# An FFT-mixing and channel-mix kernel on one Trainium2 core: mu's rows reordered behind the first sines, turn's rows on ScalarE, the feature sine first, the first half of the features ahead in two K pieces

## The chip, the cores and the metric

The kernel runs on one core of one Trainium2 chip. Its time is the device time of one execution in microseconds (us). The kernel before took a median of 431.68 us over three runs (431.59 to 433.62). A profile is one execution taken by the hardware profiler; its times count from the span's start. PE is TensorE (PEld its weight loads), DVE is VectorE, ACT is ScalarE, POOL is GpSimd, SP is SyncE, and "L757" is line 757 of the kernel.

## The reference

The input x has 8 batches of 3072 rows with 256 features. The first part is the real part of a two-dimensional Fourier transform, over the rows and over the features. The second part mixes each row of that result with the row before it, by two vectors mu_k and mu_r, and applies a gated two-layer block:

```python
X = np.fft.fft(x, axis=1)
X = np.fft.fft(X, axis=2)
x = X.real
...
xk = mu_k * x + (1.0 - mu_k) * x_prev
xr = mu_r * x + (1.0 - mu_r) * x_prev
k = np.maximum(xk @ w_k, 0.0)
v = k * k @ w_v
r = 1.0 / (1.0 + np.exp(-(xr @ w_r)))
return (r * v).astype(np.float32)
```

w_k is 256 x 1024, w_v is 1024 x 256 and w_r is 256 x 256. The result has x's shape, in float32.

## The kernel before, in words

**Transform.** The row transform is factored: x is loaded in strips and its mirrored strips are gathered by index (`load_p`, `load_m`; GpSimd issues nearly all of these transfers), both are added on VectorE (`fold`, lines 171 and 173), and TensorE multiplies the sums by a table of sines and cosines, `w_pm` (`a_sum`, line 582). `a_evac` copies the products out of PSUM as the tile `a`. Then comes the feature transform with the table `w_eo` (`d_units`, line 604; evicted as `g_all`), then the last factor of the row transform with the table `m_cs` (`c_sums`, line 646; evicted as `y`). A small permutation matrix, `turn`, mirrors one column of features (`turned`, line 627).

**Tables.** The tables are made on the chip in the first microseconds. Rows of small whole numbers are built on VectorE from an index ramp and multiplied out on TensorE as outer products (lines 334). VectorE turns the products into angles and wraps them (`ts`, line 265, used everywhere for tensor_scalar), and ScalarE takes the sine: lines 386 and 388 for `w_pm`, line 440 (`m_sine`) for `m_cs` in two parts, line 486 (`eo_sine`) for `w_eo`. The angles of the second part of `m_cs` are made on ScalarE (`m_angles_2`, line 396) and wrapped on VectorE. Line 839 then makes ScalarE load the function table with Sigmoid, which all later work uses. Two rows, TO and SG, stand in the tile `rw_turn` and become columns from which `turn` is made.

**mu.** The vectors mu_k and mu_r come by two small transfers into `mu_row`. The features sit on the partitions in the order even, odd, and mirrored for the second half, so mu is put in that order by copies on ScalarE (`mu_rows`, line 226) into `mu_p`, and TensorE turns the rows into columns (line 843).

**Mixing and the block.** `diff` subtracts neighbouring rows; `mix_part` adds mu times the difference to y. It does so either in one scalar_tensor_tensor for each half a of the features (line 738), or in two steps, `scaled` (line 711) and `mixed` (line 722). The feature contraction of w_k is in two pieces of 128, a = 0 and a = 1 (the K pieces). `k_products` (line 757) multiplies x by w_k, `k_piece` evicts with a Relu (line 767), `square` squares it on VectorE (line 777), `v_part` and `v_tile` multiply by w_v (lines 810 and 798), `r_item` makes the gate (lines 784 and 789), and `v_out` multiplies both and stores (line 820).

**Order.** Each engine's order is the program's order, pinned by `pin_order`. PSUM tiles come from two rings, three large ones (`ps_w`) and two small ones (`ps_v`); a tile can be written again when its last reader is done. The first chunk is special: its first 256 columns of `k_products` come ahead of the main loop, and of these the first four rows are mixed directly out of PSUM (lines 887 and 892). `keep_busy` (line 206) issues matmuls on zeros to fill pauses of TensorE. After the prologue, a loop of steps runs a planned list of work items.

Of the kernel before, what the change touches and what calls it, by code (L numbers as in the profile page):

```python
# [9 lines left out]
FP32 = mybir.dt.float32  # L10
# [3 lines left out]
AF = mybir.ActivationFunctionType  # L14
# [6 lines left out]
def _v(ap, extra_offset, free_dims):  # L21
    new_ap = [list(ap.ap[0])] + [[s, c] for (s, c) in free_dims]
    return dataclasses.replace(ap, offset=ap.offset + extra_offset, ap=new_ap)
# [16 lines left out]
def kernel(  # L40
# [10 lines left out]
    nc = tc.nc  # L51
# [3 lines left out]
    P = 128  # L55
# [3 lines left out]
    NJ, NJ1 = 14, 6  # L59

    const = ctx.enter_context(tc.tile_pool(name="const", bufs=1))
# [16 lines left out]
    def ps_w():  # L78
        return ps_slot("W", 3, 1024)

    def ps_v():
        return ps_slot("V", 2, 512)
# [23 lines left out]
    V = nc.vector  # L106
# [96 lines left out]
    def keep_busy(n, ps, cols=512):  # L203

        for _ in range(n):
            nc.tensor.matmul(out=ps[:, 0:cols], lhsT=zeros,
                             rhs=_v(zeros, 0, [(0, cols // P), (1, P)]), start=True, stop=True)
# [6 lines left out]

    nc.sync.dma_start(out=xp_32, in_=dataclasses.replace(x[0, 0:1, :],
                                                         ap=[[32 * D, 96], [D, 5], [1, D]]))
    mu_row = const.tile([2, 256], FP32)
    mu_p = const.tile([2, 2, P], FP32)
    unit = const.tile([2, 2], FP32)
    for i, mu in enumerate((moe_mu_k, moe_mu_r)):  # L220
        nc.scalar.dma_start(out=mu_row[i:i + 1], in_=mu.rearrange("(a b) -> a b", a=1))

    def mu_rows(a):
        for p0, f0, step, n in (((0, 0, 1, 1), (1, 2, 2, 63), (64, 1, 2, 64)),
                                ((0, 128, 1, 1), (1, 254, -2, 63), (64, 255, -2, 64)))[a]:
            nc.scalar.activation(out=mu_p[:, a, p0:p0 + n], in_=_v(mu_row, f0, [(step, n)]),
                                 func=AF.Copy)

    for h in range(2):
# [33 lines left out]
    def ts(out, in0, s1, op0, s2=None, op1=None):  # L263
        kw = {} if op1 is None else {"op1": op1}
        V.tensor_scalar(out=out, in0=in0, scalar1=s1, scalar2=s2, op0=op0, **kw)

    MUL, ADD = ALU.mult, ALU.add
# [9 lines left out]
    TO, SG = range(2)  # L277
# [5 lines left out]
    def rv(n, o, *dims, k=1):  # L283
        return _v(rw_0[0:k], P * n + o, list(dims)) if n < 6 else _v(rw_1, P * (n - 6) + o, list(dims))

    def tv(n, o, *dims):
        return _v(rw_turn, P * n + o, list(dims))

    one = ramp[0:1]
    C_0, C_1 = [(64, 2), (1, 32)], [(64, 2), (1, 32)]  # L290
# [7 lines left out]
    V.memset(rv(PH0, 64 + 47, (1, 1)), -S / 4)  # L298
    V.memset(rv(PHS0, 64 + 15, (1, 1)), S / 4)
    V.memset(rv(ONE, 0, (1, 1)), 1.0)  # L300

# [8 lines left out]
    for i in range(2):  # L312
        nc.scalar.activation(out=unit[:, i:i + 1], in_=g_i[0:2], func=AF.Copy, bias=1.0 - i,
                             scale=2.0 * i - 1.0)
    mu_rows(0)
    mu_rows(1)

    ts(rv(JR, 0, (1, P)), one, 0.0, ADD)
    ts(rv(PN, 0, (2, 64), (1, 2)), _v(one, 0, [(2, 64), (0, 2)]), 0.0, ADD)
# [49 lines left out]
    ts(ph_c, prep[:, P_C:P_C + 4], float(TURN) / S, MUL)  # L369


    V.memset(tv(SG, 0, (1, P)), 1.0)
    V.memset(tv(SG, 32, *C_1), -1.0)
    V.memset(tv(SG, 47, (64, 2)), 1.0)
    for c in range(2):
        ts(tv(TO, 32 * c, (64, 2), (1, 32)), _v(one, 32 * c, [(64, 2), (1, 32)]),
           32.0 - 64.0 * c, ADD)
    ts(tv(TO, 15, (32, 4)), _v(one, 15, [(32, 4)]), 0.0, ADD)

    ang_ps = [ps_v(), ps_v()]  # L380
    m_outer(ang_ps[0], 0, NJ1)
# [2 lines left out]
    for g in range(2):  # L384
        kw = dict(func=AF.Sin, bias=sc[:, 2 + g:3 + g], scale=sc[:, g:g + 1])
        nc.scalar.activation(out=_v(w_pm, g, [(WA + WB, 2), (2, 2), (4, NU)]),
                             in_=_v(u_w, 0, [(0, 2), (NU, 2), (1, NU)]), **kw)
        nc.scalar.activation(out=_v(w_pm, WA + g, [(WA + WB, 2), (2, NU)]),
                             in_=_v(u_w, 2 * NU, [(0, 2), (1, NU)]), **kw)

    def wrap_angles(j0, j1):
        ts(ang[:, :, j0:j1], ang[:, :, j0:j1], TURN - 1, ALU.bitwise_and)

    def m_angles_2(ps, j0, j1):
        for c in range(2):
            nc.scalar.activation(out=ang[:, c, j0:j1], in_=ps[:, 0:64 * (j1 - j0)],  # L396
                                 func=AF.Identity, bias=ph_c[:, 2 * c:2 * c + 1],
                                 scale=float(TURN) / S)

    def m_angles(ps, j0, j1, z=0):  # L400
        for c in range(2):
            for k0, k1, n in ((j0, j0 + z, 2 * c + 1), (j0 + z, j1, 2 * c))[1 - z:]:
                ts(ang[:, c, k0:k1], ps[:, 64 * (k0 - j0):64 * (k1 - j0)], float(TURN) / S, MUL,
                   ph_c[:, n:n + 1], ADD)
        if j0 == 0:
            wrap_angles(j0, j1)

    m_angles(ang_ps[0], 0, NJ1, 1)
    for c in range(2):
        ts(ueo[:, :, c], _v(prep, P_E, [(64, 2), (1, 64)]), TURN / 256.0, MUL,  # L410
           0.75 * (1 - c) * TURN, ADD)
    ts(ueo, ueo, TURN - 1, ALU.bitwise_and)
    keep_busy(NF[0], fill)

    turn = const.tile([P, P], FP16)
# [69 lines left out]
    def eo_sine():  # L485
        nc.scalar.activation(out=w_eo.rearrange("p a b -> p (a b)"),
                             in_=ueo.rearrange("p a c b -> p (a c b)"), func=AF.Sin,
                             bias=m_pi, scale=TWO_PI / TURN)
# [108 lines left out]
    def d_units(b, ps, u0, n, bank):  # L597

        for i in range(n):
            for e in range(2):
                o = bank * e + 128 * i
                nc.tensor.matmul(out=ps[:, o:o + 128],  # L604
                                 lhsT=a_t[b][:, e, 2 * (u0 + i):2 * (u0 + i) + 2, :],
                                 rhs=w_eo[:, e], start=True, stop=True)

    def d_evac(ps, u0, n, bank, eng):
        evac(_v(g_all, 256 * u0, [(64, 2), (128, 2 * n), (1, 64)]),
             _v(ps, 0, [(bank, 2), (64, 2 * n), (1, 64)]), eng)  # L610
# [8 lines left out]
    def d_small(b, u, n, eng="A"):  # L619
        ps = ps_v()  # L620
        d_units(b, ps, u, n, 256)
        d_evac(ps, u, n, 256, eng)
# [35 lines left out]
    def y_evac(b, s0, n, ps):  # L658
        o = s0 % 2
        evac(y_t[b][:, s0:s0 + n].rearrange("p s a t -> p (s a t)"),  # L660
             _v(ps, 512 * o, [(128, n // 2), (512 - 1024 * o, 2), (1, 128)]), "A")
# [62 lines left out]
                        op=ALU.subtract if m else ALU.add)  # L724

    def mix_part(b, j, lo, hi):
        if j or lo > 4:
            for a in range(2):
                scaled(b, j, 0, a, lo, hi)
            for a in range(2):  # L730
                mixed(b, j, 0, a, lo, hi)
            return


        if lo == 0:
            x_t[b, j, 0] = mix_pool.tile([P, 2, 1536], FP16, name=f"x{j}0")
        for a in range(2):
            V.scalar_tensor_tensor(out=_v(x_t[b, j, 0], 1536 * a + 64 * lo,
                                          [(64, hi - lo), (1, 64)]),
                                   in0=x_t[b][:, lo:hi, a], scalar=mu_f[:, a, j:j + 1],  # L740
                                   in1=y_t[b][:, lo:hi, a], op0=ALU.mult, op1=ALU.add)
# [4 lines left out]

    k2_t, st = {}, {}

    def k_products(c, ds, lo=0, hi=512):
        b, m, i = c  # L750
        xk = x_t[b, 0, m]
        if lo == 0:
            st["k", ds] = ps_w()
        for hs in range(2):
            fc = 2 * ds + hs
            for a in range(2):
                nc.tensor.matmul(out=st["k", ds][:, 512 * hs + lo:512 * hs + hi],  # L757
                                 lhsT=wk_sb[m][a][:, 128 * fc:128 * fc + 128],
                                 rhs=xk[:, a, 512 * i + lo:512 * i + hi],
                                 start=(a == 0), stop=(a == 1))  # L760

    def k_piece(c, ds):
        if ds == 0:
            k2_t[c] = k2_pool.tile([P, 8, 512], FP16, name="k2", tag="k2")
            st["rl"] = k2_pool.tile([P, 8, 512], FP16, name="rl", tag="rl")
        k_products(c, ds, 256 if c == chunks[0] and ds < 2 else 0)
        nc.scalar.activation(out=st["rl"][:, 2 * ds:2 * ds + 2],  # L767
                             in_=st["k", ds].rearrange("p (f t) -> p f t", f=2),
                             func=AF.Relu, bias=0.0, scale=0.25)
# [59 lines left out]

    m_angles_2(ang_ps[1], NJ1, NJ)
    ts(w_pm[:, 0:2, WA:WA + WB], w_pm[:, 0:2, WA:WA + WB], math.sqrt(0.5), MUL)
    ts(w_pm[:, 2], w_pm[:, 0], -1.0, MUL)
    wrap_angles(NJ1, NJ)
    m_sine(0, NJ1)
    eo_sine()
    m_sine(NJ1, NJ)
    nc.scalar.activation(out=warm, in_=zeros[:, 0:1], func=AF.Sigmoid)  # L839
    fold(0, 0, 1, 4)  # L840
# [30 lines left out]
    w, first = ps_w(), ps_w()  # L871
# [13 lines left out]
    for a in range(2):  # L885
        t = x_t["t", a] = mix_pool.tile([P, 24, 64], FP16, name=f"t{a}")
        nc.scalar.activation(out=t[:, 0:4],
                             in_=_v(first, 64 * a, [(128, 2), (512, 2), (1, 64)]), func=AF.Copy,
# [39 lines left out]
    chunks = [(b, m, i) for b in range(B) for m in range(2) for i in range(3)]  # L928
# [16 lines left out]
    for n, c in enumerate(chunks[:EARLY]):  # L945
        o_steps[4 * n + SHORT + 3] = [(c, 1, 2), (c, 3, 2)]
    o_steps[4 * EARLY + SHORT + 3] = [(chunks[EARLY], 1, 2)]
    k_products(chunks[0], 0, 0, 256)
    k_products(chunks[0], 1, 0, 256)
    diff(0, 4, 8)  # L950
    mix_part(0, 0, 4, 8)
    d_small(0, 8, 2)
    d_small(0, 10, 2)
    y_evac(0, 0, 4, first)
    diff(0, 8, 16)
    at(0, mix_part, 0, 0, 8, 16)
    at(0, diff, 0, 0, 4)
# [71 lines left out]
    for b in range(B):  # L1029
# [9 lines left out]
        if t < B:  # L1039
# [6 lines left out]
            c = [(c_pairs, t, 8 * n, (8, 8, 8, 4)[n], EV[n]) for n in range(4)]  # L1046
# [75 lines left out]
```

## Time and profile before

| what | value |
| --- | --- |
| median of three runs | 431.68 us (431.59 to 433.62) |
| profiled execution, its own time | 431.61 us |
| its span | 429.8 us |
| busy share of the span | PE 98%, DVE 84%, ACT 74%, POOL 15% |
| granted TensorE clock | 1.000 |
| moved by DMA | 42.06 MB, mean 98 GB/s |

The span runs from the first to the last instruction; 1.8 us of the profiled execution's time lie around it. In the views that follow, a row of a timeline begins with its start and its length in us, then engine, line, operation, the tiles written and read, shapes and count; consecutive equal instructions are merged into one row, and the bracket at the end says how long the engine was idle before and what ended that. A row of the chain of waits begins with start and length of a link. A row of waits reads: who waited, for whom, us in total, times, longest. A row of DMA issues ends with the time from issue to landing. A row of groups reads: count, busy us in all, mean ns of one, idle before.

### The profile page before, as it was taken

To read this page: it belongs to the slowest core of one execution; us is meant where nothing else is said; L and a number is where in the kernel's file an instruction comes from. 1 tells how busy PE (TensorE), PEld (TensorE's weight loads), DVE (VectorE), ACT (ScalarE), POOL (GpSimd) and SP (SyncE) were. 2 spreads that over 40 slices of the span, in tenths; PEclk is the share of its full clock that TensorE was granted. 3 is DMA by queue.
4 is the path that set the end of the run, shared out by engine and by line. 5 is a ranking of instruction groups with operands and counts; after the bars stand their busy time and mean duration, and the time that the engine had idled before them with its cause. 6 is when DMAs were issued, how large, how long until landed. Compare 5 with 4: busy or idle time off the path is not lost.

```text
span 429.8 us, 9301 instructions
## 1 busy us (share of the span) xinstructions
PE 422.9 (98%) x3858; PEld 298.0 (69%) x3858; DVE 360.9 (84%) x547; ACT 320.2 (74%) x373; POOL 63.4 (15%) x96
## 2 busy tenths in 40 slices
PE   8999999999999999999999999999999999999996
PEld 3667776777777776776677777777767767766765
DVE  8899989997998889988898988989799847997453
ACT  7889897877878678776777777777786767666661
POOL 7686302000050002300041000500000000000000
PEclk9999999999999999999999999999999999999999
DMA  8999917322286233933269223763232322223233
GB/s 169 134 152 207 231 48 129 76 56 68 71 147 150 51 76 63 191 93 72 58 115 188 57 55 72 135 157 75 53 72 50 76 64 61 70 64 72 67 74 98
DMA packets 35103, 42.06 MB, mean 98 GB/s; under 512 B 4115, under 2 KB 31093, under 8 KB 35061
## 3 DMA queue, kind: packets, MB, share of 16 engines
q1 hardware_dynamic: 27488, 25.41, 23.7%
q0 software_dynamic: 7264, 15.80, 22.5%
q8 instruction: 30, 0.49, 0.5%
q10 hardware_dynamic: 308, 0.26, 0.2%
q14 instruction: 13, 0.10, 0.1%
HBM read 32.08 MB, written 25.17 MB: 133 GB/s over the span
## 4 chain that ended last, share of the span: by engine, by line
PE 94%; ACT 3%; DVE 1%; DMA 1%; issue 0%; ACTq 0%
PE psW L757 39%; PE psV L798 36%; PE psW L784 10%; PE psV L810 3%; PE psW L604 2%; PE psW L678 1%; PE psW L564 1%; DMA mu_row<-in_moe_mu_r_dram 1%; PE psW L646 1%; ACT a L521 1%; ACT m_cs L440 0%; PE psW L582 0%; ACT L839 0%; DVE x L892 0%; ACT rl L396 0%; ACT rl L767 0%
## 5 line engine op out<-in xcount | busy, mean ns | idle before, releaser
L767 ACT ACTIVATE rl<-psW 128x1024 f16<-128x1024 f32 x192 | 195.2, 1025 | 92.5 <-PE psW L757 89.0
L757 PE MATMUL psW<-x,wk 128*128 128x512 f16 (+1 forms) x776 | 195.7, 377 | 0.5
L798 PE MATMUL psV<-wv_sb,k 128*128 128x256 f16 x1424 | 184.1, 273 | 0.0
L798 PEld LDWEIGHTS <-k 128*128 128x128 f16 x1424 | 136.8, 98 | 35.9
L777 DVE TENSOR_TENSOR k<-rl 128x2048 f16<-128x2048 f16 (+1 forms) x101 | 116.3, 1152 | 33.4 <-ACT rl L767 33.0
L757 PEld LDWEIGHTS <-wk 128*128 128x128 f16 x776 | 74.8, 98 | 53.5 <-issue 1.3
L820 DVE SCALAR_TENSOR_TENSOR o<-psV,r 128x512 f32<-128x512 f32 (+1 forms) x97 | 65.8, 681 | 15.1 <-PE psV L798 13.5
L722 DVE TENSOR_TENSOR x<-y,t 128x1536 f16<-128x1536 f16 (+2 forms) x72 | 61.6, 860 | 2.1
L784 PE MATMUL psW<-wr,x 128*128 128x256 f16 x384 | 49.8, 273 | 0.0
L789 ACT ACTIVATE r<-psW 128x1024 f16<-128x1024 f32 x48 | 48.9, 1019 | 0.8 <-PE psW L784 0.8
L784 PEld LDWEIGHTS <-x 128*128 128x128 f16 x384 | 37.4, 98 | 14.4 <-issue 0.2
L463 POOL IOTA gate<- 1x1 int32 x6 | 2.1, 356 | 199.4 <-DVE gate L462 199.4
L521 ACT ACTIVATE a<-psW 128x832 f16<-128x832 f32 x31 | 25.9, 862 | 1.4 <-PE psW L564 1.4
L521 ACT ACTIVATE g_all<-psW 128x1024 f16<-128x1024 f32 (+5 forms) x37 | 25.6, 695 | 0.4 <-PE psW L627 0.2
L140 POOL DMA_INDIRECT xm<-in_x_dram,idx_g x18 | 24.2, 1344 | 5.5 <-issue 5.5
L171 DVE TENSOR_TENSOR p<-xp,xm 112x2304 f16<-112x2304 f16 (+6 forms) x19 | 21.6, 1139 | 0.0
L711 DVE TENSOR_SCALAR t<-d,muf_t 128x1536 f16<-128x1536 f16 (+2 forms) x40 | 20.8, 529 | 0.0
L711 DVE TENSOR_SCALAR t<-d,mu_m 128x1536 f16<-128x1536 f16 x32 | 19.6, 614 | 0.0
L604 PEld LDWEIGHTS <-a 128*128 128x128 f16 x208 | 14.0, 98 | 6.6 <-ACT a L521 0.6
L182 DVE TENSOR_TENSOR eo<-p 112x1152 f16<-112x1152 f16 (+3 forms) x28 | 17.9, 679 | 0.0
L521 ACT ACTIVATE pq<-psW 128x1024 f16<-128x1024 f32 (+1 forms) x18 | 15.2, 879 | 2.3 <-PE psW L678 2.3
L699 DVE TENSOR_TENSOR d<-y 128x1664 f16<-128x1664 f16 (+5 forms) x19 | 16.7, 880 | 0.0
(137 smaller groups left out, 217.7 us busy)
## 6 DMA issues: line engine op xcount, KB each, us to landing
out_dram<-o SPq DMA_DIRECT2D x189, 128.0 KB, 2.4
xp<-in_x_dram POOLq DMA_DIRECT2D x12, 216.0 KB, 4.5
xp<-in_x_dram POOLq DMA_DIRECT2D x13, 192.0 KB, 7.4
xp<-in_x_dram POOLq DMA_DIRECT2D x2, 384.0 KB, 6.9
wv_sb<-in_moe_w_v_dram POOLq DMA_DIRECT2D x1, 512.0 KB, 8.2
xp<-in_x_dram SPq DMA_DIRECT2D x1, 480.0 KB, 4.7
xp<-in_x_dram POOLq DMA_DIRECT2D x1, 432.0 KB, 6.4
xm<-in_x_dram,idx_g POOLq DMA_INDIRECT x18, 7.9
```

The source lines that it names most:

```text
L140: nc.gpsimd.indirect_dma_start(dst, None, src, bass.IndirectOffsetOnAxis(ap=idx, axis=0))
L521: nc.scalar.activation(out=out_ap, in_=in_ap, func=AF.Copy)
L604: nc.tensor.matmul(out=ps[:, o:o + 128], lhsT=a_t[b][:, e, 2 * (u0 + i):2 * (u0 + i) + 2, :], rhs=w_eo[:, e], start=True, stop=True)
L711: V.tensor_scalar(out=dst, in0=src, scalar1=mu, scalar2=None, op0=ALU.mult)
L722: V.tensor_tensor(out=_v(x_t[b, j, m], o, [(64 * step, hi - lo), (step, 64)]), in0=y_t[b][:, lo + 3 * m:hi + 3 * m, a], in1=x_t["t", a][:, ...
L757: nc.tensor.matmul(out=st["k", ds][:, 512 * hs + lo:512 * hs + hi], lhsT=wk_sb[m][a][:, 128 * fc:128 * fc + 128], rhs=xk[:, a, 512 * i + l ...
L767: nc.scalar.activation(out=st["rl"][:, 2 * ds:2 * ds + 2], in_=st["k", ds].rearrange("p (f t) -> p f t", f=2), func=AF.Relu, bias=0.0, sca ...
L777: V.tensor_tensor(out=k2_t[c][:, lo:hi], in0=r, in1=r, op=ALU.mult)
L784: nc.tensor.matmul(out=ps[:, 256 * tb:256 * tb + 256], lhsT=x_t[b, 1, m][:, a, 512 * i + 128 * tb: 512 * i + 128 * tb + 128], rhs=wr_sb[m] ...
L789: nc.scalar.activation(out=st["r", c], in_=ps, func=AF.Sigmoid)
L798: nc.tensor.matmul(out=st["v", tb - h][:, 256 * h:256 * h + 256], lhsT=k2_t[c][:, fc, 128 * tb:128 * tb + 128], rhs=wv_sb[:, fc], start=(f ...
L820: V.scalar_tensor_tensor(out=o.rearrange("p a b -> p (a b)")[:, 0:256 * n], in0=st["v", t0][:, 0:256 * n], scalar=16.0, in1=st["r", c][:, ...
```

## The change

Six edits, all ahead of or at the very beginning of the main loop:

- `mu_row` is one column wider. `mu_rows` is three copies instead of six: one copies mu's element 128 behind the row's end, then one strided copy for each half writes all 128 values. It is called behind the sines of `w_pm`, ahead of `m_angles_2`, where it stood ahead of them.
- SG's three memsets on VectorE stand earlier, with the other rows; TO's three rows are made on ScalarE instead of VectorE.
- VectorE makes the feature angles `ueo` ahead of `m_angles`, and wraps the second part's angles ahead of the scaling of `w_pm`; ScalarE takes the feature sine ahead of `m_cs`.
- `mix_part` for rows 4 to 8 of the first chunk uses two scalings and two additions instead of two scalar_tensor_tensor.
- The first 256 and the second 256 columns of the first two `k_products` of the first chunk are issued by K piece: a = 0 for both PSUM tiles, then a = 1. In the second 256 columns the last piece of the second tile stands behind the first tile's Relu in the program.
- `y_evac(0, 0, 4, first)` is issued ahead of two `d_small` instead of behind them.

```diff
-    mu_row = const.tile([2, 256], FP32)
+    mu_row = const.tile([2, 257], FP32)
...
-        nc.scalar.dma_start(out=mu_row[i:i + 1], in_=mu.rearrange("(a b) -> a b", a=1))
-
-    def mu_rows(a):
-        for p0, f0, step, n in (((0, 0, 1, 1), (1, 2, 2, 63), (64, 1, 2, 64)),
-                                ((0, 128, 1, 1), (1, 254, -2, 63), (64, 255, -2, 64)))[a]:
-            nc.scalar.activation(out=mu_p[:, a, p0:p0 + n], in_=_v(mu_row, f0, [(step, n)]),
+        nc.scalar.dma_start(out=mu_row[i:i + 1, 0:256], in_=mu.rearrange("(a b) -> a b", a=1))
+    def mu_rows():
+        nc.scalar.activation(out=mu_row[:, 256:257], in_=mu_row[:, 128:129], func=AF.Copy)
+        for a in range(2):
+            nc.scalar.activation(out=mu_p[:, a], in_=_v(mu_row, 256 * a, [(1 - 2 * a, 2),
+                                                                         (2 - 4 * a, 64)]),
                                  func=AF.Copy)
...
+    V.memset(tv(SG, 0, (1, P)), 1.0)
+    V.memset(tv(SG, 32, *C_1), -1.0)
+    V.memset(tv(SG, 47, (64, 2)), 1.0)
...
-    mu_rows(0)
-    mu_rows(1)
...
-    V.memset(tv(SG, 0, (1, P)), 1.0)
-    V.memset(tv(SG, 32, *C_1), -1.0)
-    V.memset(tv(SG, 47, (64, 2)), 1.0)
     for c in range(2):
-        ts(tv(TO, 32 * c, (64, 2), (1, 32)), _v(one, 32 * c, [(64, 2), (1, 32)]),
-           32.0 - 64.0 * c, ADD)
-    ts(tv(TO, 15, (32, 4)), _v(one, 15, [(32, 4)]), 0.0, ADD)
+        nc.scalar.activation(out=tv(TO, 32 * c, (64, 2), (1, 32)),
+                             in_=_v(one, 32 * c, [(64, 2), (1, 32)]), func=AF.Copy,
+                             bias=32.0 - 64.0 * c)
+    nc.scalar.activation(out=tv(TO, 15, (32, 4)), in_=_v(one, 15, [(32, 4)]), func=AF.Copy)
...
-    m_angles(ang_ps[0], 0, NJ1, 1)
     for c in range(2):
         ts(ueo[:, :, c], _v(prep, P_E, [(64, 2), (1, 64)]), TURN / 256.0, MUL,
            0.75 * (1 - c) * TURN, ADD)
     ts(ueo, ueo, TURN - 1, ALU.bitwise_and)
+    m_angles(ang_ps[0], 0, NJ1, 1)
...
-        if j or lo > 4:
+        if j or lo:
...
-    def k_products(c, ds, lo=0, hi=512):
+    def k_products(c, ds, lo=0, hi=512, halves=(0, 1)):
...
-        if lo == 0:
+        if lo == 0 and halves[0] == 0:
...
-            for a in range(2):
+            for a in halves:
...
+    def k_early(lo, hi, which):
+        for a, ds in which:
+            k_products(chunks[0], ds, lo, hi, (a,))
...
-        k_products(c, ds, 256 if c == chunks[0] and ds < 2 else 0)
+        if c == chunks[0] and ds < 2:
+            if ds == 0:
+                k_early(256, 512, ((0, 0), (0, 1), (1, 0)))
+            else:
+                k_early(256, 512, ((1, 1),))
+        else:
+            k_products(c, ds)
...
+    mu_rows()
     m_angles_2(ang_ps[1], NJ1, NJ)
+    wrap_angles(NJ1, NJ)
     ts(w_pm[:, 0:2, WA:WA + WB], w_pm[:, 0:2, WA:WA + WB], math.sqrt(0.5), MUL)
     ts(w_pm[:, 2], w_pm[:, 0], -1.0, MUL)
-    wrap_angles(NJ1, NJ)
+    eo_sine()
     m_sine(0, NJ1)
-    eo_sine()
     m_sine(NJ1, NJ)
...
-    k_products(chunks[0], 0, 0, 256)
-    k_products(chunks[0], 1, 0, 256)
+    k_early(0, 256, ((0, 0), (0, 1), (1, 0), (1, 1)))
     diff(0, 4, 8)
     mix_part(0, 0, 4, 8)
+    y_evac(0, 0, 4, first)
     d_small(0, 8, 2)
     d_small(0, 10, 2)
-    y_evac(0, 0, 4, first)
```

## The prediction

> **What bounds the kernel now.** I read the page first, then the chain of waits over the first 50 us, then the waits, and last each engine's order of time and the DMA landings.
>
> ```profile
> span 429.8 us, 9301 instructions
> PE 94%; ACT 3%; DVE 1%; DMA 1%; issue 0%; ACTq 0%
> ...
> PEld L810 <- DVE k L777: 0.5, 1, 0.5
> ```
>
> The chain that ends last runs on TensorE for 94% of the span. The whole edit lies ahead of that stretch, so it is worth only what it moves the moment at which TensorE stops waiting. The chain of waits says where that is (start, length, what):
>
> ```profile
> 7.00 1.12 ACT rl L396 x2
> ...
> 10.40 1.28 ACT L839
> ...
> 17.38 1.13 DVE x L892 x4
> ...
> 20.41 0.93 PE psW L757 x7
> ...
> 23.32 1.05 PE psV L810 x8
> ```
>
> Read naively, ScalarE carries the first part, and everything taken off it is gain. The wait row above warns against that for the end of the stretch: the last thing that TensorE waits for in the prologue is the square on VectorE in front of the matmuls of line 810 at 23.32.
>
> **The sines move forward.** ScalarE sat still for 1.10 us, then copied six rows of mu, then began the sines:
>
> ```profile
> 4.72 0.89 ACT L226 ACTIVATE mu_p<-mu_row 2x1 f32<-2x1 f32 x6 [1.10 <-DMA mu_row<-in_moe_mu_r_dram]
> 5.51 0.61 ACT L386 ACTIVATE w_pm<-u_w,sc 128x104 f16<-128x104 int32 x1
> ...
> 2.44 0.15 DVE L265 TENSOR_SCALAR g_i<-pcol_i 128x1 int32<-128x1 int32 x1 [0.24 <-POOL pcol_i L244]
> ...
> 4.06 0.20 DVE L265 TENSOR_SCALAR u_w<-u_w 128x78 int32<-128x78 int32 x1
> ...
> 4.29 0.17 DVE L372 MEMSET rw_turn<- 1x128 f16 x1
> ...
> 4.70 0.06 DVE L374 MEMSET rw_turn<- 1x2 f16 x1
> ...
> 7.81 0.60 PE L843 MATMUL psV<-unit,mu_p 2*128 2x2 f32 x4
> ```
>
> Without the copies the first sine waits for u_w, done at 4.26. The three SG memsets now stand ahead of u_w: from 4.29 to about 4.76 they took 0.47 with their own waits, and VectorE has a hole of 0.24 there (its wait for pcol_i), so u_w slips by at most 0.23, to 4.5. The sine can start near 4.55 instead of 5.51: 0.96 earlier. The three TO copies on ScalarE fit between 3.62 (4.72 less the 1.10) and 4.5 (a small copy costs 0.89/6 = 0.15, three 0.45): nothing on the path. Their price if that hole were gone is 0.45.
>
> The three mu copies then come back behind the sines. By the same row they cost 0.45, and up to 0.2 more because two of them read the column that the first one writes. So the reorder is worth 0.96 less 0.45 to 0.65, some 0.3 to 0.5, at line 396 and down to the table load of line 839. Behind them in ScalarE's queue wait the angles, the sines and all evictions; TensorE wants mu_p at 7.81 and gets it near 6.6. The feature sine ahead of the others, the angles of ueo ahead of m_angles and the second wrap ahead of the w_pm scaling change only which input is ready first: all are ready before ScalarE asks, so I cost them at nothing.
>
> **What is late next.** The gain has to pass the x data. The folds of batch 0's second half and their gathers:
>
> ```profile
> 4.68 0.95 POOL L140 DMA_INDIRECT xm<-in_x_dram,idx  x1 [0.30 <-issue]
> 5.94 0.91 POOL L140 DMA_INDIRECT xm<-in_x_dram,idx  x1 [0.30 <-issue]
> ...
> xm<-in_x_dram,idx POOLq DMA_INDIRECT x1, 6.2
> ...
> xm<-in_x_dram,idx POOLq DMA_INDIRECT x1, 5.8
> ...
> 11.02 0.68 DVE L171 TENSOR_TENSOR p<-xp,xm 96x1024 f16<-96x1024 f16 x1
> 11.82 0.68 DVE L171 TENSOR_TENSOR p<-xp,xm 96x1024 f16<-96x1024 f16 x1
> ...
> 12.82 1.06 PE L582 MATMUL psV<-w_pm,p 96*128 96x208 f16 x10
> ...
> 14.04 0.56 ACT L521 ACTIVATE a<-psV 128x416 f16<-128x416 f32 x1
> ...
> 14.65 0.40 PE L604 MATMUL psV<-w_eo,a 128*128 128x128 f16 x4
> ```
>
> The two landing rows are those of the gathers issued at 4.68 and 5.94. They land at 4.68 + 6.2 = 10.88 and 5.94 + 5.8 = 11.74, and the folds that read them start at 11.02 and 11.82: 0.14 and 0.08 later. These folds cannot come forward by more than that, and the second not at all once the hand-over is counted. Nothing in the edit touches GpSimd's queue ahead of them. So the ten matmuls of line 582 still run from 12.82 to 13.88, and the last eviction of a, which ScalarE reached at 14.04, can start at 13.88 plus a hand-over of 0.04 to 0.05 (14.60 to 14.65 is such a one). **Of 0.3 to 0.5 us, 0.12 is left.** From here to the mixing at 17.38 one engine waits for the next, and 0.12 is passed on whole.
>
> **The four-step mix.** At 19.47 two scalar_tensor_tensor become two scalings and two additions. VectorE runs without a hole from 17.38 to the square that releases TensorE, so here each nanosecond counts:
>
> ```profile
> 19.47 0.88 DVE L738 SCALAR_TENSOR_TENSOR x<-d,muf_t,y 128x256 f16<-128x256 f16 x2
> 20.27 0.69 DVE L699 TENSOR_TENSOR d<-y 128x1024 f16<-128x1024 f16 x1
> ...
> 23.80 0.61 DVE L711 TENSOR_SCALAR t<-d,muf_t 128x512 f16<-128x512 f16 x2
> ...
> 25.00 0.68 DVE L777 TENSOR_TENSOR k<-rl 128x1024 f16<-128x1024 f16 x1
> ...
> L711 DVE TENSOR_SCALAR t<-d,muf_t 128x512 f16<-128x512 f16 x10 | 3.1, 349 | 0.0
> L711 DVE TENSOR_SCALAR t<-d,mu_m 128x1536 f16<-128x1536 f16 x4 | 2.4, 612 | 0.0
> L699 DVE TENSOR_TENSOR d<-y 128x512 f16<-128x512 f16 x2 | 0.8, 414 | 0.0
> L699 DVE TENSOR_TENSOR d<-y 128x256 f16<-128x256 f16 x1 | 0.3, 282 | 0.0
> ```
>
> The pair takes 20.27 - 19.47 = 0.80 start to start. The same four-step form at 512 columns takes 25.00 - 23.80 = 1.20. Halving saves 0.414 - 0.282 = 0.13 for each addition, and for each scaling (0.612 - 0.349)/1024 x 256 = 0.07. That gives 1.20 - 0.26 - 0.14 = 0.80 to, with rounding and one more wait of a VectorE instruction for the one before it, 0.88; I take 0.84, **0.04 lost**. Bounds: 1.20 if nothing shrinks (0.40 lost); 1.20 - 4 x 0.13 = 0.68 if scalings shrink like additions (0.12 gained).
>
> [...]
>
> **The two K pieces and the earlier y eviction.** Now four matmuls with the first half of the features run before the second half of x is there. In the first 256 columns the second psum tile is asked for two matmuls sooner; queued behind it are the second half's matmuls, whose x comes at 17.38 + 1.13 = 18.51 anyway. In the second 256 columns the first half of x is there after three of the four steps, some 0.64 behind their start, near 20.0; at 0.93/7 = 0.13 a matmul all eight are through near 21.1, where they ended at 20.41 + 0.93 = 21.34. The first relu needs six of them and could start near 20.9 instead of 21.19, since the eviction of y is out of its way too. But its consumer is the square, and VectorE gets to that in its own order:
>
> ```profile
> 21.19 1.96 ACT L767 ACTIVATE rl<-psW 128x1024 f16<-128x1024 f32 x2
> ...
> 22.25 0.41 DVE L699 TENSOR_TENSOR d<-y 128x512 f16<-128x512 f16 x1
> 22.59 1.29 DVE L777 TENSOR_TENSOR k<-rl 128x1024 f16<-128x1024 f16 x2
> ```
>
> The first relu was over by about 22.2 (half of the pair's 1.96) and the square started at 22.59 directly behind the subtraction at 22.25. The relu was not what it waited for; an earlier one brings nothing. Cost and gain: nothing, hidden by VectorE's backlog. If that backlog were gone, the piece could be worth at most the 0.5 that the weight load of line 810 waits for the square in the first fence.
>
> **Sum.** 0.12 gained, 0.04 lost: 0.08 us. The profiled execution took 431.61 us (span 429.8 and 1.8 around it) and lies 0.07 under the median of 431.68. 431.61 - 0.08 = 431.53, I say **431.5**.
>
> **Rivals.**
> *The landings do not hold it* (chance 0.17). If the x gathers come a little earlier than this execution shows, the folds follow VectorE. The second wrap must wait for line 396, which is 0.3 to 0.5 earlier, and the folds get about 0.24 of that. Then the last eviction gains 0.12 + 0.24 = 0.36 and the sum is 431.61 - 0.36 + 0.04 = 431.3. For it: only 0.08 separates landing and fold, and landings can shift. Against it: GpSimd's queue is the same, and so are its transfers.
>
> *The four steps cost what they cost at 512 columns* (chance 0.16), slower than before. Place: VectorE between 19.47 and 20.27. Price up to 0.40; 431.61 - 0.12 + 0.40 = 431.9. It decides from 0.12 on, where it eats the gain. For it: the chain on VectorE has no hole until the square. Against it: the additions' rows do shrink with their columns.
>
> *TensorE starts with a slow clock for longer* (chance 0.07). The rows for equal fillers early and late:
>
> ```profile
> 0.99 1.89 PE L206 MATMUL psW<-zeros 128*128 128x512 f16 x4 [0.99 <-DVE xm L234]
> 5.75 2.14 PE L206 MATMUL psW<-zeros 128*128 128x512 f16 x8
> 8.40 1.04 PE L206 MATMUL psW<-zeros 128*128 128x512 f16 x4
> 10.28 1.70 PE L582 MATMUL psW<-w_pm,p 96*128 96x208 f16 x16 [0.85 <-DVE p L173]
> ```
>
> Four fillers take 1.89 at first and 1.04 later, 0.21 more each. The SG memsets make TensorE's first rows up to 0.2 later, so a pause is added while it still runs slowly; if the eight fillers at 5.75 stay slow, 8 x 0.21 = 1.7 is lost, of which 0.85 is covered by the wait at 10.28: 431.61 + 0.85 - 0.08 = 432.4. [...]
>
> **How the numbers follow.** The forecast has 0.55, the rivals 0.17, 0.16 and 0.07; 0.05 is left for what I do not see. The range takes in the first two rivals, the bounds of the four-step mix and the third rival's near end: 430.8 to 432.5. About 0.5% (2.2 us) is what a measurement of this kernel tells from no change. To be faster than that, more would have to vanish than the whole 1.10 wait plus the copies, so 0.03; slower needs the slow clock for all twelve fillers or something unseen, 0.05; within 0.5%: 0.92.
>
> **What would show it.** The first w_pm sine near 4.5 and the table load 0.3 to 0.5 earlier than 10.40 (first step). The fold now at 11.82 still there while ScalarE idles ahead of the last eviction of a, which starts near 13.92 (second). Four instructions on VectorE in 0.84 where the pair took 0.80 (third). The relu earlier by more than the square (fourth), and line 810 starting near 23.24. It is wrong if the fold moves with the sines, if line 810 starts before 23.0 or after 23.5, or if TensorE is held again later than that.

## The result, and the profile after

Measured beside each other, the kernel before took a median of 431.88 us (431.54 to 433.62, 14 runs) and the changed one 433.43 us (431.96 to 433.72, 14 runs): ratio 1.0024, 95% interval 1.0014 to 1.0035. The change costs 1.5 us by the medians and 1.0 by the ratio. Within 0.5% this is no change, as forecast; the forecast time of 431.5 is missed by 1.9 us, and 433.43 lies outside its 430.8 to 432.5. The profiled execution of the changed kernel took 432.41 us and is a mild one: 11 of the 14 took 433.05 or more.

These are the rows of the changed kernel's profile that the prediction used. The page first, with its shares of the chain of work that ended last:

```profile
span 430.6 us, 9300 instructions
PE 98%; DVE 1%; issue 0%; ACT 0%; POOL 0%
```

As before, what lies ahead of TensorE's long stretch is all that counts. ScalarE's order of time (start, length, then the instruction):

```profile
4.55 0.62 ACT L388 ACTIVATE w_pm<-u_w,sc 128x104 f16<-128x104 int32 x1 [0.39 <-DVE u_w L268]
...
5.94 0.18 ACT L226 ACTIVATE mu_row<-mu_row 2x1 f32<-2x1 f32 x1
6.03 0.51 ACT L228 ACTIVATE mu_p<-mu_row 2x128 f32<-2x128 f32 x2
6.44 1.23 ACT L398 ACTIVATE rl<-psV,ph_c 128x512 int32<-128x512 f32 x2
...
9.96 1.28 ACT L853 ACT_TABLE_LOAD   x1
...
14.19 0.55 ACT L523 ACTIVATE a<-psV 128x416 f16<-128x416 f32 x1
...
21.92 1.94 ACT L780 ACTIVATE rl<-psW 128x1024 f16<-128x1024 f32 x2 [0.85 <-PE psV L606]
```

The first sine is at 4.55, the table load 0.44 earlier than it was (10.40). Then the gain is gone: the last eviction of a starts at 14.19, later than the 14.04 of before, and the first squared relu at 21.92 instead of 21.19, after 0.85 of idling. TensorE's rows:

```profile
6.07 3.28 PE L206 MATMUL psW<-zeros 128*128 128x512 f16 x8
...
10.74 1.59 PE L584 MATMUL psW<-w_pm,p 96*128 96x208 f16 x16
...
23.85 1.04 PE L823 MATMUL psV<-wv_sb,k 128*128 128x256 f16 x8
```

The eight fillers took 3.28 where they took 2.14. Until 8.63 they start 0.43 apart, and the trace's record of the full granted clock begins at 8.88; in the trace of the kernel before it begins at 6.23, and the fillers start 0.43 apart ahead of that and 0.22 behind it. Line 584 (582 before) starts 0.46 later than it did. Line 823 (810 before) starts at 23.85 instead of 23.32, outside the 23.0 to 23.5 that the prediction set as its own test.

### The profile page after: what moved, and what is told of

It reads as the page before. It is cut to its first block, busy times and chain, and to the rows that moved or that the text cites. A ratio compares the mean times of both kernels' runs of the same rounds, so it can differ in the third digit from the quotient of the medians.

```text
span 430.6 us, 9300 instructions
## 1 busy us (share of the span) xinstructions
PE 423.7 (98%) x3858; PEld 299.1 (69%) x3858; DVE 360.8 (84%) x546; ACT 320.7 (74%) x373; POOL 63.7 (15%) x96
## 4 chain that ended last, share of the span: by engine, by line
PE 98%; DVE 1%; issue 0%; ACT 0%; POOL 0%
PE psW L759 39%; PE psV L811 36%; PE psW L797 10%; PE psV L823 3%; PE psW L606 2%; PE psW L680 1%; PE psW L566 1%; PE psW L206 1%; PE psW L584 1%; PE psW L648 1%; PE psV L338 1%; PE psV L606 0%; ACT rl L780 0%; PE psV L584 0%; DVE g_all L521 0%
## 5 line engine op out<-in xcount | busy, mean ns | idle before, releaser
L724 DVE TENSOR_TENSOR x<-y,t 128x1536 f16<-128x1536 f16 (+3 forms) x74 | 62.0, 845 | 2.1
L713 DVE TENSOR_SCALAR t<-d,muf_t 128x1536 f16<-128x1536 f16 (+3 forms) x42 | 21.2, 516 | 0.1
```

The lines of the kernel that those rows point to most:

```text
L713: V.tensor_scalar(out=dst, in0=src, scalar1=mu, scalar2=None, op0=ALU.mult)
L724: V.tensor_tensor(out=_v(x_t[b, j, m], o, [(64 * step, hi - lo), (step, 64)]), in0=y_t[b][:, lo + 3 * m:hi + 3 * m, a], in1=x_t["t", a][:, ...
```

## Experiments

Eighteen runs were made in seven sets, four of them of the changed kernel itself; the kernels of a set ran on one chip in turn with the kernel before, so each row is read against the before of its own set (the later expectations call a set an allocation). The numbers are medians in us, of 12 executions and of 17 to 35 of before, the ratio with its 95% interval, and the span of the profiled execution.

| set | kernel | median | before | ratio | span |
| --- | --- | --- | --- | --- | --- |
| 1 | e1_again, as changed | 431.51 | 431.73 | 0.9990 (0.9978 to 1.0002) | 429.4 |
| 1 | e2_tables, front alone | 431.24 | 431.73 | 0.9989 (0.9978 to 1.0000) | 429.4 |
| 1 | e3_pieces, pieces, mix, y alone | 431.70 | 431.73 | 0.9995 (0.9979 to 1.0011) | 429.8 |
| 1 | e4_sg_back | 431.69 | 431.73 | 0.9996 (0.9983 to 1.0008) | 430.1 |
| 2 | e6_again2, as changed | 433.34 | 432.20 | 1.0020 (1.0005 to 1.0035) | 432.4 |
| 2 | e7_holes | 433.30 | 432.20 | 1.0014 (0.9999 to 1.0029) | 431.5 |
| 2 | e8_four | 433.37 | 432.20 | 1.0034 (1.0015 to 1.0054) | 432.6 |
| 2 | e5_sg_early | 432.04 | 432.20 | 0.9990 (0.9976 to 1.0005) | 430.1 |
| 3 | e9_again3, as changed | 431.57 | 431.73 | 0.9984 (0.9971 to 0.9996) | 429.6 |
| 3 | e10_tables2, front alone | 431.30 | 431.73 | 0.9983 (0.9970 to 0.9996) | 429.4 |
| 3 | e11_pieces2 | 431.65 | 431.73 | 0.9992 (0.9979 to 1.0004) | 430.0 |
| 3 | e12_order | 431.43 | 431.73 | 0.9983 (0.9971 to 0.9995) | 430.2 |
| 4 | e13_again4, as changed | 431.74 | 431.73 | 0.9991 (0.9980 to 1.0002) | 430.4 |
| 4 | e14_tables3, front alone | 431.54 | 431.73 | 0.9991 (0.9981 to 1.0001) | 429.4 |
| 4 | e15_pieces3 | 431.59 | 431.73 | 0.9989 (0.9976 to 1.0003) | 429.8 |
| 5 | e16_tables4, front alone | 431.85 | 432.20 | 0.9985 (0.9974 to 0.9997) | 430.9 |
| 6 | e17_order2 | 431.52 | 432.04 | 0.9986 (0.9974 to 0.9997) | 429.8 |
| 7 | e18_order3 | 433.00 | 431.77 | 1.0021 (1.0009 to 1.0034) | 431.5 |

The same program is 0.2 us faster than before in sets 1 and 3, level with it in set 4, and 1.1 to 1.5 us slower in set 2 and in the first measurement. So there are two questions: what is different in those two, and which part of the change pays for it.

**Set 1: the parts.** Two theories were put up after the result. Late clock: TensorE keeps its slow clock for longer (the fillers' 3.28), and this pushes back all that follows. Late relu: the new order of the pieces with the earlier y delays the first squared relu. e1_again is the changed kernel unchanged.

> The changed kernel as it is, a second profile. Late clock (my theory: the SG memsets ahead make TensorE's first rows 0.2 us later and open pauses, so that its clock opens one stretch later; the fillers of line 206 then run slowly and push the prologue): the profile shows the eight fillers at 0.43 us each for longer than to 8.9 us, the first a-matmuls of line 584 later than 10.74, and the median is near 433.4. Late relu (rival: the order by K pieces makes the first relu and the square late, as at 21.9 in the first profile): the relu is late by 0.7 us again in a slow and in a quick execution alike.

Neither loss came: the median is 0.22 under before, with an interval that just takes in no change. TensorE's and ScalarE's order of time in e1_again:

```profile
6.07 2.06 PE L206 MATMUL psW<-zeros 128*128 128x512 f16 x8
...
10.13 1.69 PE L584 MATMUL psW<-w_pm,p 96*128 96x208 f16 x16 [0.45 <-DVE p L173]
...
22.93 1.05 PE L823 MATMUL psV<-wv_sb,k 128*128 128x256 f16 x8
```

```profile
13.70 0.55 ACT L523 ACTIVATE a<-psV 128x416 f16<-128x416 f32 x1
...
20.72 1.94 ACT L780 ACTIVATE rl<-psW 128x1024 f16<-128x1024 f32 x2 [0.28 <-PE psW L759]
```

Here the fillers take 2.06, the last eviction of a starts 14.04 - 13.70 = 0.34 earlier than before and line 823 starts 23.32 - 22.93 = 0.39 earlier; the span is 0.4 shorter. The folds, in VectorE's order of e1_again:

```profile
10.86 0.68 DVE L171 TENSOR_TENSOR p<-xp,xm 96x1024 f16<-96x1024 f16 x1
...
11.65 0.68 DVE L171 TENSOR_TENSOR p<-xp,xm 96x1024 f16<-96x1024 f16 x1
```

They stand back to back behind their predecessor, 0.16 and 0.17 earlier than before: the landings did not hold them. (The landings that the prediction computed, 10.88 and 11.74, come from times given to a tenth, so the 0.14 and 0.08 that it left the folds were within the rounding.) e2_tables undoes the pieces, the mix and the place of y; e3_pieces undoes the rest.

```diff
 # e2_tables
-        if j or lo:
+        if j or lo > 4:
...
-        if c == chunks[0] and ds < 2:
...
+        k_products(c, ds, 256 if c == chunks[0] and ds < 2 else 0)
...
-    k_early(0, 256, ((0, 0), (0, 1), (1, 0), (1, 1)))
+    k_products(chunks[0], 0, 0, 256)
+    k_products(chunks[0], 1, 0, 256)
     diff(0, 4, 8)
     mix_part(0, 0, 4, 8)
-    y_evac(0, 0, 4, first)
     d_small(0, 8, 2)
     d_small(0, 10, 2)
+    y_evac(0, 0, 4, first)
```

> Only the edits up to the sines (mu, SG, TO, the order of angles and sines); the K pieces, the four-step mix and the place of the y eviction as before. Late clock: as slow as the whole change, 433.2 to 433.6. Late relu: 431.4 to 431.8, no slower than before.

> Only the K pieces, the four-step mix and the earlier y eviction; all edits up to the sines as before. Late clock: like before, 431.4 to 431.9. Late relu: slower than before by 0.5 to 1.6.

The front alone has the whole gain (span 429.4, the same as e1_again), the pieces with mix and y none (429.8, as before). Neither theory's number for these two came (433.2 to 433.6 for the front, 0.5 to 1.6 slower for the pieces); but as the changed kernel lost nothing in this set either, that does not yet tell what loses in the other measurements. e4_sg_back is the changed kernel with SG's memsets back in their old place.

> The whole change, with the three SG memsets back behind ph_c on VectorE. Late clock: TensorE's rows start at 2.92 and 3.53 again, the clock opens near 6.2 and the median is 431.3 to 431.8. Late relu: 433.2 to 433.6, like the whole change.

Its profile shows what a late landing does. The fold in its VectorE order:

```profile
11.53 0.69 DVE L171 TENSOR_TENSOR p<-xp,xm 96x1024 f16<-96x1024 f16 x1 [0.69 <-DMA xm<-in_x_dram,idx]
```

In that execution a gather came later, the fold waited 0.69 for it, and the span was 430.1. So the landings can hold the gain, as the prediction said, but did so in this profile alone of set 1.

**Set 2: the clock is not it.** e6_again2 is the changed kernel again. e7_holes adds a filler in each of two pauses, meant to open the clock earlier (its eight fillers took 1.89); e8_four halves the eight fillers; e5_sg_early is the kernel before with the SG memsets early.

```diff
 # e7_holes
-    keep_busy(4, fill)
+    keep_busy(5, fill)
...
     outer(prep[:, P_E:P_E + 128], (row(JR, P), rv(JR, 0, (1, 2), (2, 64), k=P)))
+    keep_busy(1, fill)
 # e8_four
-    NF = (8, 4,
+    NF = (4, 4,
```

> The changed kernel unchanged, a third time. The executions of one kernel spread over 431.2 to 432.4, with a second group at 433.0 to 433.7; the change had 11 of 14 there at first and none of 12 the second time. [...] Late relu: the first relu at 21.9 again whenever the time is above 432.

> The whole change with two more fillers of TensorE, one behind the first four and one between the small outer products and the two of line 338, in the pauses at 2.9 and 3.6 us. Late clock: fewer pauses, so the clock opens by 7.8 us at the latest, nearly all executions lie at 431.1 to 431.6 and none at 433 and over. Late relu: no difference from the change itself.

> The whole change with four fillers in place of eight behind the outer products. Late clock: if it is the slow fillers that push the a-matmuls, each filler taken away gives 0.43 us back when the clock is late, so the slow group shrinks or vanishes; if the fillers are what opens the clock, there are more executions at 433 and over, since TensorE then pauses ahead of the a-matmuls. Late relu: no difference from the change itself.

> The kernel before with nothing but the three SG memsets moved ahead. Late clock: TensorE's rows start at 3.10 and 3.85 as in the change; the share of executions at 433 and over rises from the 7 of 35 of the kernel before, and the rest stays at 431.5 to 431.9 because the sines still wait for mu. Late relu: like before.

The loss is there again in e6_again2; e8_four has as much; the early SG memsets alone (e5_sg_early) have none, though the eight fillers took 2.67 there. e8_four's clock opened late as well: its four fillers at 8.91 still took 1.89, as long as the first four of all. But e7_holes has the loss with an early clock: its fillers start 0.22 apart from 5.86 on, ahead of the 7.8 of the expectation, which is the author's estimate and which no run shows. It is the useful one, because from 10 us on VectorE's rows up to 24.6 and TensorE's up to 25.8 stand within 0.02 of e1_again's. (A line was added, so each of its lines is one higher.) VectorE in e1_again, then in e7_holes:

```profile
24.62 0.68 DVE L790 TENSOR_TENSOR k<-rl 128x1024 f16<-128x1024 f16 x1
25.22 0.25 DVE L505 CAST w_hh<-psW 112x104 f16<-112x104 f32 x1
25.39 0.68 DVE L790 TENSOR_TENSOR k<-rl 128x1024 f16<-128x1024 f16 x1
```

```profile
24.61 0.68 DVE L791 TENSOR_TENSOR k<-rl 128x1024 f16<-128x1024 f16 x1
27.02 0.27 DVE L506 CAST w_hh<-psW 112x104 f16<-112x104 f32 x1 [1.73 <-ACT g_all L524]
27.20 0.68 DVE L791 TENSOR_TENSOR k<-rl 128x1024 f16<-128x1024 f16 x1
```

VectorE's queue is stopped for 1.73 us at w_hh, a copy of 0.27, because ScalarE's small copy g_all is late. ScalarE in e1_again, then in e7_holes:

```profile
22.81 1.96 ACT L780 ACTIVATE rl<-psW 128x1024 f16<-128x1024 f32 x2
24.62 0.24 ACT L523 ACTIVATE g_all<-psW 128x5 f16<-128x5 f32 x1
```

```profile
22.88 1.04 ACT L781 ACTIVATE rl<-psW 128x1024 f16<-128x1024 f32 x1
24.49 1.02 ACT L781 ACTIVATE rl<-psW 128x1024 f16<-128x1024 f32 x1 [0.56 <-PE psW L503]
26.80 0.19 ACT L524 ACTIVATE g_all<-psW 128x5 f16<-128x5 f32 x1 [1.29 <-remote]
```

And what ScalarE waited for, TensorE in e7_holes:

```profile
5.86 1.89 PE L206 MATMUL psW<-zeros 128*128 128x512 f16 x8
...
21.87 1.02 PE L760 MATMUL psW<-x,wk 128*128 128x512 f16 x4
22.92 1.05 PE L824 MATMUL psV<-wv_sb,k 128*128 128x256 f16 x8
23.81 0.17 PE L630 MATMUL psW<-g_all,turn 128*128 128x5 f16 x1
23.84 0.32 PE L503 MATMUL psW<-w_pm,order 96*112 96x52 f16 x3
...
27.04 0.40 PE L649 MATMUL psW<-m_cs,g_all 64*128 64x128 f16 x8 [0.83 <-ACT g_all L524]
```

The matmuls for the relu at 24.49 ended at 21.87 + 1.02 = 22.89. g_all's one, line 630, updates no semaphore itself; the three of line 503 behind it do, and ended at 23.84 + 0.32 = 24.16. Both ends are as in e1_again to 0.08 us. Yet ScalarE went on 1.6 and 2.6 us later; ahead of the relu it was busy until 23.9, so 0.56 and 1.29 of that are idle time. The fillers had taken 1.89 there, so the clock was open early. Late clock falls as the cause of this loss: the time goes between TensorE's rows and the engines that wait for them, in updates that come late. The wait outlasted the end of the rows by 0.04 us where ScalarE followed at once (line 759 in e1_again, 25.02 to 25.06) and by up to 2.6 here. The trace of the profile after records such updates themselves: those for the eight rows that end from 19.91 to 26.12 us are 0.30 to 1.29 behind those ends, where in the trace of the kernel before every one between 19 and 34 us is 0.01 to 0.02 behind.

How does the loss get back to TensorE? The last row of the fence above and one of the waits say it:

```profile
PE psW L649 <- ACT y L524: 0.9, 1, 0.9
```

TensorE itself waited for ScalarE, 0.83 for g_all and 0.9 for a later eviction of y, which had again waited for late updates (1.2): 1.7 together, of the 2.1 by which its span is longer than e1_again's. VectorE's stop at w_hh has the same cause, but does not stand on the chain of waits there, which goes from the relu to g_all, line 649 and y. Late relu, as it was put, falls too: the first relus of e7_holes are on time and the loss comes at the fourth and behind it.

The share of the work done between 22 and 34 us shows the size. The rows of the view by stretches (length, then busy us and instructions of PE, PEld, DVE, ACT, POOL, the granted clock, and the share and GB/s of DMA) for e1_again and for e7_holes:

```profile
22.00:34.00 12.00, 11.89 (x100) 7.73 (x99) 11.90 (x31) 9.92 (x13) 10.04 (x17) 1.00 0.94 154
34.00:84.00 50.00, 49.88 (x496) 36.02 (x494) 46.88 (x71) 43.20 (x50) 10.88 (x12) 1.00 0.65 138
```

```profile
22.00:34.00 12.00, 10.23 (x85) 6.45 (x84) 9.97 (x24) 8.19 (x11) 10.14 (x17) 1.00 1.04 174
34.00:84.00 50.00, 49.88 (x495) 35.90 (x494) 46.90 (x76) 43.01 (x49) 11.47 (x13) 1.00 0.65 132
```

VectorE does 11.90 - 9.97 = 1.9 us less work in that stretch and nothing is lost later: TensorE is busy 49.88 of the next 50 us in both. The spans differ by 431.5 - 429.4 = 2.1.

**Sets 3 and 4: which part.** The new theories: Pieces, the reordered first chunk lets the late updates in; Front, the earlier tables do. e9_again3 and e13_again4 are the changed kernel, e10_tables2 and e14_tables3 the front alone, e11_pieces2 and e15_pieces3 the pieces, mix and y alone. e12_order is the changed kernel with the old order of the first chunk's products:

```diff
 # e12_order (and e17_order2, e18_order3)
-    k_early(0, 256, ((0, 0), (0, 1), (1, 0), (1, 1)))
+    k_products(chunks[0], 0, 0, 256)
+    k_products(chunks[0], 1, 0, 256)
...
-        if c == chunks[0] and ds < 2:
-            if ds == 0:
-                k_early(256, 512, ((0, 0), (0, 1), (1, 0)))
-            else:
-                k_early(256, 512, ((1, 1),))
-        else:
-            k_products(c, ds)
+        k_products(c, ds, 256 if c == chunks[0] and ds < 2 else 0)
```

> The changed kernel unchanged, as the measure for the three beside it. In two earlier profiles of it, and in two variants, TensorE's semaphore updates reach ScalarE up to 1.7 us after the matmul's end between 20 and 30 us, and about 2 us are lost there; in another of the same kernel every update is 0.01 us behind and nothing is lost. Theory Pieces: the new order of the first chunk's pieces is what lets late updates into the path. Theory Front: the earlier front is what does it, since it shifts the first squared relus against the loads. Both expect here either about 433.3 (1.2 over before, relus 2 to 4 idle for over 0.5 us each, ahead of 30 us) or, where the updates are in time, about 431.3 (0.4 under before).

> The new front alone (tables, mu, sines), the first chunk's products, mix and y as before. Pieces: no loss, 0.3 to 0.5 under before, whatever the changed kernel beside it does. Front: the same loss as the changed kernel beside it, within 0.4 us. If the updates are in time on this chip, both expect 0.4 under before, and the run tells nothing.

> The new pieces, four-step mix and earlier y alone, the front as before. Pieces: the same loss as the changed kernel beside it, within 0.4 us. Front: as before within 0.3 us. If the updates are in time, both expect it within 0.2 of before.

> The changed kernel with the first chunk's products again grouped by feature pair (both K halves of one pair, then of the other); the four-step mix and the earlier y stay. Pieces: the loss is gone (0.3 to 0.5 under before) while the changed kernel beside it has it. Front: the loss stays, within 0.4 of the changed kernel. If the updates are in time, both expect 0.4 under before.

> The changed kernel unchanged. It came out 1.2 to 1.5 over before in two measurements, with TensorE's semaphore updates up to 1.8 us behind the matmuls between 20 and 30 us, and 0.2 under before in two others, with every update 0.01 us behind. Both theories expect one of these two again, about 433.3 or about 431.5, and that the trace shows which by the lateness of the updates.

> The new front alone. Where the updates are late: theory Pieces expects it within 0.5 of the before of this call, theory Front the loss of the changed kernel beside it (over 1.0 over before). Where they are in time: 431.3 by both.

> The new pieces, mix and earlier y alone. Where the updates are late: theory Pieces expects the loss of the changed kernel beside it (over 1.0 over before), theory Front within 0.5 of before. Where they are in time: 431.7 by both.

In neither set were the updates late, so neither theory was tested. What the sets do show is the parts again: the front alone 429.4 in both, the pieces 430.0 and 429.8 against 429.8 before. And they show the slow clock by itself, in e13_again4 (the view ends at 12 us, in the midst of the last row):

```profile
6.08 3.62 PE L206 MATMUL psW<-zeros 128*128 128x512 f16 x8
...
11.09 1.15 PE L584 MATMUL psW<-w_pm,p 96*128 96x208 f16 x11
```

Against e1_again the fillers took 1.56 longer, line 584 starts 0.96 later, and the span is 430.4 - 429.4 = 1.0 longer.

**Sets 5 to 7: front, order, and what is left.** One kernel each: the front alone, then twice the changed kernel with the old order of the products.

> The new front alone, measured by itself, to meet an allocation in which TensorE's updates are late. Where the trace shows them up to 1.8 us late between 20 and 30 us: theory Front expects it over 1.0 over the before of this call (the changed kernel had 1.2 and 1.5), theory Pieces within 0.5 of it. Where they are in time: 431.3 to 431.5 by both, 0.2 to 0.4 under before.

> The changed kernel with the first chunk's products grouped by feature pair again; the new front, the four-step mix and the earlier y stay. The front alone stayed 0.35 under before where the updates are late, so the loss is of the pieces or of the y with the mix. Where the trace shows late updates: theory Order (the K halves in a new order move the late updates onto ScalarE's second and third squared relu) expects the loss gone, 0.1 to 0.5 under before; theory Early y (the earlier y and the mix do it) expects 1.0 to 1.5 over before. Where they are in time: 431.4 by both.

> The changed kernel with the first chunk's products grouped by feature pair again, a third time, for an allocation with late updates. Theory Order there: 0.1 to 0.5 under before. Theory Early y there: 1.0 to 1.5 over before. Where the updates are in time: 431.4 to 431.6 by both, and the question stays open.

In set 6 the updates were in time, and nothing is told apart there. In sets 5 and 7 they were late. The waits of e16_tables4 have this row (who, for whom, us in total, times, longest):

```profile
ACT rl L769 <- PE psV L812: 1.0, 1, 1.0
```

and its chain of waits this link:

```profile
30.53 0.86 PE psW L759 x4
```

The relu for these matmuls waited 1.0 us, though they ended at 30.53 + 0.86 = 31.39: the row names line 812, whose matmuls stand behind them. Its g_all and its w_hh were not late, on ScalarE and on VectorE:

```profile
23.92 1.98 ACT L769 ACTIVATE rl<-psW 128x1024 f16<-128x1024 f32 x2
25.73 0.26 ACT L523 ACTIVATE g_all<-psW 128x5 f16<-128x5 f32 x1
```

```profile
26.26 0.25 DVE L505 CAST w_hh<-psW 112x104 f16<-112x104 f32 x1
```

and the front alone stays 0.35 us under the before of its set. e18_order3 has w_hh as e7_holes has it:

```profile
24.89 1.02 ACT L769 ACTIVATE rl<-psW 128x1024 f16<-128x1024 f32 x1 [0.49 <-PE psW L502]
27.13 0.19 ACT L523 ACTIVATE g_all<-psW 128x5 f16<-128x5 f32 x1 [1.22 <-remote]
```

```profile
27.35 0.27 DVE L505 CAST w_hh<-psW 112x104 f16<-112x104 f32 x1 [1.51 <-ACT g_all L523]
```

and loses 1.2 us. It differs from e16_tables4 only in the place of the y eviction and in the four-step mix. The loss needs no new order of the products, so theory Order falls; the front alone did not have it, so Front by itself falls. What is left is Early y: the y eviction ahead of the two `d_small`, or the four steps, or both, perhaps only together with the front. Every profile of a kernel with these two edits where updates were late has the wait at w_hh (0.3 in the profile after, 0.8 in e6_again2, 1.7 in e7_holes and in e8_four, 1.5 in e18_order3); the two without them, e5_sg_early and e16_tables4, have none. In those two profiles the updates ahead of g_all and w_hh were in time, though; the late ones came elsewhere. So Early y is what the runs point to, and it is not shown: no set with late updates had both the front alone and a kernel with these edits, the pieces, mix and y without the front never met late updates (e3_pieces, e11_pieces2, e15_pieces3), and the two edits were not separated. Nor does the wait at w_hh measure the loss: e6_again2 has a span of 432.4 with 0.8 there, and its TensorE waited 1.2 for a relu instead.

## Why the prediction was wrong, point by point

- **Sines forward: right.** First sine 4.55 as said; the mu copies cost 6.44 - 5.94 = 0.50, in 0.45 to 0.65 (the up to 0.2 for reading the first copy's column was the author's estimate, and 0.05 came); the table load came 0.44 earlier, in 0.3 to 0.5.
- **"What is late next": mis-sized.** The step let 0.12 of the gain through. Where TensorE's clock opened early, e1_again measured 0.34 at the last eviction and 0.39 at line 823. That is the rival "the landings do not hold it", which said 0.36, with 0.24 for the folds, for which it shows no row and which measured 0.16 and 0.17. Its 431.3 is near what the front alone measured where the updates were in time (431.24, 431.30, 431.54). The landings are not fixed from execution to execution: in e4_sg_back the fold waited 0.69 for one, in e1_again none waited.
- **The four-step mix: right in its own price.** Its first row in the profile after and the row behind the last:

```profile
19.62 0.48 DVE L713 TENSOR_SCALAR t<-d,muf_t 128x256 f16<-128x256 f16 x2
20.02 0.49 DVE L724 TENSOR_TENSOR x<-y,t 128x256 f16<-128x256 f16 x2
20.43 0.68 DVE L701 TENSOR_TENSOR d<-y 128x1024 f16<-128x1024 f16 x1
```

  20.43 - 19.62 = 0.81 against 0.80 for the pair; 0.84 was forecast.
- **"The two K pieces and the earlier y eviction": this step failed.** It said "Cost and gain: nothing, hidden by VectorE's backlog", and that the most it could be worth without the backlog was a gain of 0.5. In sets with updates in time that holds: with the pieces the first relu was at 20.72 and line 823 at 22.93, and the front alone had the same span. Where the updates come late it does not: the kernels with the earlier y and the mix lost 1.1 to 1.5 us. VectorE's backlog does not cover what TensorE takes straight from ScalarE. In e7_holes TensorE waited 0.83 for g_all and 0.9 for y, and VectorE, whose backlog ends at w_hh behind g_all, stood still for 1.7. The prediction had no bound on the loss side for this step, reckoned with hand-overs from TensorE of 0.04 to 0.05 us alone, and looked for the cover at the first square only. That the loss goes with the earlier y or the mix is argued from e16_tables4 and e18_order3; what makes the updates late, and why the wait then stands at g_all and w_hh, stays open.
- **The rival of the slow clock: the slow clock did last longer in some executions, and it is not what the medians show.** The early SG memsets move the fillers from 5.75 to 6.07, by 0.32 where 0.2 was allowed. The eight then took 3.28 in the profile after, 3.62 in e13_again4, but 2.06 in e1_again with the same memsets, so that the later start alone delays the clock is not shown. With SG late they took 2.02 to 2.47 in five profiles (before, e3_pieces, e4_sg_back, e11_pieces2, e15_pieces3). (The kernel before's own change lies at 6.23: its first two fillers start 0.43 apart, the third 0.25 behind the second, the later ones 0.22 apart.) The price is 0.96 at line 584, near the 0.85 said. It explains 0.5 us of the profile after (14.19 against 13.70 at the last eviction) and the 1.0 of e13_again4's span, but not 433.4: e7_holes measured 433.30 with the fillers at 1.89.

## What to carry to other kernels

A cost of nothing behind one engine's backlog holds only for what passes through that engine, and only up to where the backlog ends: look for the first places behind it where a short hand-over between two other engines stands on the path (here g_all, which waits for TensorE and for which TensorE waited 0.83 and VectorE 1.73 us in e7_holes), and price a late hand-over there. Where a change is worth a few tenths of a us, measure its parts in several sets, since the same program came out 0.2 under and 1.5 over. The best version measured of these is the front alone, at or below the changed kernel in each set that had both and 0.2 to 0.5 us below before in four sets, though two of these four intervals reach no change; with the SG memsets also back in their place it was not tried.

## What the runs showed of the hardware

- **TensorE's updates came late in some executions, and ScalarE went on up to 2.6 us after its rows' end** (e7_holes, 24.16 to 26.80). Late ones lie between 20 and 34 us of the span, in the first measurement's profile (0.30 to 1.29 us) and in sets 2, 5 and 7. In e1_again, from a set without the loss, ScalarE's waits for the matmuls of line 759 ended 0.04 us behind them. It does not go with the chip's number: sets 2, 3 and 6 have the same one on record, and only set 2 had late updates. The trace of the profile after also lacks records: counted in it, 452 semaphore updates of TensorE against 458 in that of the kernel before, and, more clearly, 3923 updates by landing DMA transfers against 4116. Whether the recording itself holds TensorE up, no run shows, and why these sets differ stays open.
- **The moment at which TensorE's clock opens differs in one program from execution to execution.** The same eight fillers took 2.06, 3.28, 3.58 and 3.62 us in four of the five profiles of the changed kernel, and 1.89 once two more fillers stood ahead of them. In the profile after the record of the full granted clock begins at 8.88, and the fillers start 0.43 apart until then. In e1_again the second filler starts 0.38 behind the first and the others about 0.22 apart; in e13_again4 all eight start 0.43 apart, the last at 9.1. By this spacing the clock opened near 6.4 us in one and behind 9.0 in the other. Why the moment varies, no run shows.
- **The kernel before loses time in another way too.** In the seven sets 45 of its 185 executions had a granted clock of 0.995 or 0.996 and took 432.88 us or more, and so had 7 of 36 of the pieces, mix and y alone, but none of the 48 each of the changed kernel and of the front alone, whose clock was 0.997 to 1.000. No profile shows such an execution, so why is open.
